# One PSUM tile for the 64-row jobs and another pairing of batches, in the last stage of an attention and spectral-mixing kernel

## The chip, the cores and the metric

The kernel runs on one core of one Trainium2 chip. The metric is the device time of one execution in microseconds (us); smaller is better. PE is the matmul engine, ACT and DVE are the two engines that read sums out of PSUM here, SyncE (SP) and GpSimd (POOL) issue the DMA transfers of this stage.

## The reference, cut to what matters

```python
# B = 8 batches, 8 heads x 64, S = 576 rows, D = 512
x   = attention_with_forget_decay(q, k, v, f)      # (B, S, D); cut
X   = np.fft.rfft(x, axis=1)[:, :64]               # 64 modes along the rows
Y   = X @ (w_r + 1j * w_i)                         # one D x D matrix per mode
u   = x + np.fft.irfft(Y, n=S, axis=1)
out = u + np.maximum(u @ w_ch, 0.0)                # float32, 9.44 MB
```

All weights have been read and all modes are done when the stage begins. What is left per row is `u = x + (inverse transform)` and `z = u @ w_ch`, which PE forms as sums in PSUM, the copy of u, `max(z, 0) + u`, and the store.

## The kernel before: the parts that the change and the argument touch

A batch has 576 rows: four blocks of 128 rows (`sb` 0 to 3) and a last one of 64 rows (`sb` 4). A *job* is one or two such blocks. I number the 20 jobs from 0.

```python
psPair = [{"u": psE, "z": psE}, {"u": psU}]     # "z" of the second pair: psX, added later

def start(n, tags="uz"):                        # PSUM tiles of job n, two banks each
    return [
        psPair[n % 2][tag].tile([128, 2, D], F32, tag=tag, name="p" + tag)
        for tag in tags
    ]

def wide(job):                                  # same block of two batches
    return len(job) == 2 and job[0][0] != job[1][0]

def emit_u(job, ps, u, split=False):            # ACT: u out of PSUM
    ...
        nc.scalar.copy(u[:, bs, :], ps[0][:, bs, :])

def emit_o(job, ps, u, o, pair, split=False):   # DVE, then SyncE's store
    for i in range(2 if split else 1):          # split: job 0 only, in two halves
        ...
        nc.vector.scalar_tensor_tensor(
            o[:, bs, :], ps[1][:, bs, :], 0.0, u[:, bs, :], ALU.max, ALU.add
        )
        b, sb = job[0]
        n_wide = 4 * (b // 2 - 1) + sb          # which wide job this is
        if sb == 4:
            ...                                 # single: two stores of 128 KB
        elif not wide(job):
            ...                                 # narrow pair: stored alone
        elif sb % 2 or n_wide < 2:              # wide: held for the next job,
            ...                                 #   but for the first two

jobs = []
for b in range(0, B, 2):
    if b == 0:
        jobs += [((c, sb), (c, sb + 1)) for c in (b, b + 1) for sb in (0, 2)]
    else:
        jobs += [((b, sb), (b + 1, sb)) for sb in range(4)]
    jobs.append(((b, 4),))

def late_rows(t, src):      # the last rows of Y, for u (t = 0) and for z (t = 1)
    keep(nc.vector.tensor_copy(yls[0][:, t, :], src))
    keep(nc.vector.tensor_copy(row_slot(0, t, H2, H4), yls[0][0:H4, t, :]))
    for b in (1, 2):        # 16 KB each, from one place in SBUF to another
        emit_moves(yls[0], H2, b, t, nc.sync)
    for b in (3, 4):
        emit_moves(yls[0], H2, b, t, nc.gpsimd)
... # batches 5 to 7: nc.gpsimd, afterwards

for n, job in enumerate(jobs):
    zs = terms(job, ps, 1, ...)                 # PE work of z of job n
    ...
        nxt = start(n + 1)
        us = terms(jobs[n + 1], nxt, 0, "xy")   # and of u of job n + 1
    ... # run zs and us, in an order that depends on the kind of job
        emit_u(jobs[n + 1], nxt, uo_n[0])
    emit_o(job, ps, *uo, n == 0)
```

The *small moves* in `late_rows` carry each batch's last rows of Y to the partitions where PE reads them. SyncE issues four of them, in the order: batch 1 for u, batch 2 for u, batch 1 for z, batch 2 for z.

The softmax here doesn't subtract the row's maximum and nothing guards it: scores larger than these inputs give would overflow.

## Time and profile before

| | before |
|---|---|
| time, median of 3 runs | 436.66 us (436.33 to 436.97) |
| the profiled run: time, span of its trace | 436.95 us, 435.2 us |
| last sum of the modes, where the stage starts (DVE writes YT) | 400.63 us |
| from there to the end of the span | 34.57 us |
| from there to the end of DVE's last step | 26.51 us |

Whole traces shift by a microsecond from one execution to the next ahead of the last stage (it starts between 400.11 and 401.81 in the traces of this study), so I count from the last write of YT wherever two traces are compared.

Of this stage the start, on DVE (columns: start, duration, engine, line, operation, output<-inputs, shape, count; in brackets the idle time before it and what ended it):

```profile
400.63 0.23 DVE L153 TENSOR_TENSOR YT<-A,Yacc 128x64 bf16<-128x64 f32 x1 [2.10 <-PE A L172]
...
403.99 2.52 DVE L1005 SCALAR_TENSOR_TENSOR uo<-pz,uo 128x512 f32<-128x512 f32 x3 [0.77 <-DMA yy<-yl]
406.71 1.23 DVE L1005 SCALAR_TENSOR_TENSOR uo<-pz,uo 128x1024 f32<-128x1024 f32 x1 [0.20 <-ACT uo L1000]
408.12 1.82 DVE L1005 SCALAR_TENSOR_TENSOR uo<-pz,uo 128x1024 f32<-128x1024 f32 x2 [0.19 <-PE pz L828]
410.48 4.67 DVE L1005 SCALAR_TENSOR_TENSOR os<-pz,us 128x1024 f32<-128x1024 f32 x4 [0.54 <-issue]
```

The first of the lower lines is jobs 0 and 1, the next two are jobs 2 and 3 (batch 1 alone) with the first single, the last is jobs 5 to 8. Job 2 waits only for ACT. The small moves do not appear as a wait after 403.99. In the DMA view of the stretch from 403.5 to 403.9, the third and the fourth small move of SyncE need 1.8 us from issue to landing (columns: tiles, queue, operation, count, size, median us to landing):

```profile
yy<-yl SPq DMA_DIRECT2D x2, 16.0 KB, 1.8
```

The same view from 402 to 407 has GpSimd's moves of the same size beside them:

```profile
yy<-yl POOLq DMA_DIRECT2D x10, 16.0 KB, 3.1
yy<-yl SPq DMA_DIRECT2D x4, 16.0 KB, 1.8
```

### The profile page before, as it was taken

Reading aid. Unit: us, or ns where it says so; the run is one execution under the profiler, and the core shown is the slowest. Engines: PE = TensorE matmul, PEld = TensorE weight load, DVE = VectorE, ACT = ScalarE, POOL = GpSimd, SP = SyncE. Lnnn points to the kernel's source line nnn. Section 1 sums busy time; section 2 is a strip of 40 time slices with the busy share of each in tenths; the row PEclk is TensorE's granted clock in tenths of the full one; section 3 lists DMA queues with packets and bytes.
Section 4 is the critical chain, followed back from the end, with each engine's and each line's share of the span. In section 5 each row is a group of like instructions: output and inputs, shape, how many; then the busy total and the mean of one; then the engine's idle time right before and its main releaser. Section 6 shows DMA issues by size and latency. Waiting matters only on the chain.

```text
span 435.2 us, 12314 instructions
## 1 busy us (share of the span) xinstructions
PE 368.1 (85%) x5313; PEld 249.7 (57%) x5313; DVE 263.7 (61%) x659; ACT 224.4 (52%) x339; POOL 126.8 (29%) x198
## 2 busy tenths in 40 slices
PE   3787799999987879778787788799999998899881
PEld 2454566776666666566565666656665555454540
DVE  5797888876555655555557568533332665553892
ACT  2887488774526454365462646134434443631781
POOL 8333332333233233232333222223223223200400
PEclk9996899996558665586565869589999999989997
DMA  8999999999999999999999999999999999995797
GB/s 184 234 235 241 234 236 238 235 212 236 234 215 236 225 224 237 210 238 233 214 237 211 212 211 212 211 211 211 211 211 211 212 210 211 211 211 100 253 367 274
DMA packets 50982, 97.38 MB, mean 224 GB/s; under 512 B 3792, under 2 KB 12976, under 8 KB 50928
## 3 DMA queue, kind: packets, MB, share of 16 engines
q0 software_dynamic: 46560, 86.09, 100.9%
q1 hardware_dynamic: 4368, 10.51, 6.7%
q8 instruction: 41, 0.67, 0.6%
q14 instruction: 13, 0.11, 0.1%
HBM read 163.73 MB, written 9.44 MB: 398 GB/s over the span
## 4 chain that ended last, share of the span: by engine, by line
PE 35%; DMA 26%; ACT 12%; DVE 10%; issue 4%; SPq 0%; DVEq 0%; POOL 0%; ACTq 0%
DMA wb<-in_moe_w_i_dram 25%; ACT E L576 8%; PE pav L614 7%; PE ps L569 7%; PE A L188 6%; PE tp L307 5%; PE px L657 2%; PE vp L541 2%; DVE QTs L322 2%; ACT KT L320 2%; ACT VT L326 2%; DVE XT L671 1%; DVE os L1005 1%; DVE E L591 1%; PE px L682 1%
## 5 line engine op out<-in xcount | busy, mean ns | idle before, releaser
L576 ACT ACTIVATE E<-ps 128x1024 bf16<-128x1024 f32 (+1 forms) x128 | 101.5, 851 | 26.1 <-PE ps L569 15.4
L93 POOL DMA_DIRECT2D wb<-in_moe_w_r_dram x64 | 42.5, 664 | 128.9 <-PE A L188 25.1
L188 PE MATMUL A<-XT,wb 128*128 128x16 bf16 x1984 | 69.9, 181 | 8.2 <-DMA wb<-in_moe_w_i_dram 3.8
L188 PEld LDWEIGHTS <-wb 128*128 128x128 bf16 x1984 | 63.5, 100 | 22.8 <-issue 11.9
L569 PE MATMUL ps<-QTs,KT 64*128 64x64 bf16 (+4 forms) x384 | 60.2, 334 | 16.6 <-ACT E L576 14.7
L93 POOL DMA_DIRECT2D wb<-in_moe_w_i_dram x64 | 42.3, 661 | 77.5 <-DMA wb<-in_moe_w_i_dram 32.5
L614 PE MATMUL pav<-va,E 128*128 128x65 bf16 (+1 forms) x1088 | 57.1, 214 | 3.2 <-DVE x_all L636 2.6
L614 PEld LDWEIGHTS <-E 128*128 128x128 bf16 (+1 forms) x1088 | 47.0, 118 | 16.9 <-issue 7.0
L591 DVE TENSOR_TENSOR E<-E,trimask 128x256 bf16<-128x256 bf16 (+2 forms) x128 | 36.9, 303 | 20.0 <-ACT E L576 19.8
L326 ACT COPY VT<-tp 128x640 bf16<-128x640 bf16 (+1 forms) x32 | 23.2, 761 | 33.4 <-PE tp L307 33.4
L867 ACT CAST XW<-pxw 128x512 bf16<-128x512 f32 x36 | 20.7, 586 | 35.9 <-PE pxw L860 28.3
L569 PEld LDWEIGHTS <-KT 64*128 64x128 bf16 x384 | 19.4, 100 | 33.6 <-issue 22.8
L860 PE MATMUL pxw<-wch,yy 128*128 128x512 bf16 x144 | 36.0, 388 | 0.0
L320 ACT COPY KT<-tp 128x640 bf16<-128x640 bf16 (+1 forms) x32 | 21.9, 749 | 26.0 <-PE tp L307 25.8
L910 ACT CAST XW<-pB 128x512 bf16<-128x512 f32 x36 | 21.0, 585 | 25.4 <-PE pB L828 25.3
L909 DVE CAST x_all<-pA 128x512 bf16<-128x512 f32 x36 | 24.9, 692 | 14.2 <-PE pA L828 12.5
L322 DVE COPY QTs<-tp 128x640 bf16<-128x640 bf16 (+1 forms) x32 | 23.4, 767 | 14.3 <-PE tp L307 14.0
L636 DVE TENSOR_TENSOR x_all<-pav,rcp 128x384 bf16<-128x384 f32 x64 | 29.1, 455 | 0.9
L625 DVE RECIPROCAL rcp<-pav 128x6 f32<-128x6 f32 x64 | 12.1, 189 | 25.1 <-PE pav L614 24.3
L828 PEld LDWEIGHTS <-ident_bf 64*64 64x64 bf16 (+1 forms) x348 | 15.7, 108 | 17.9 <-issue 9.3
L153 DVE TENSOR_TENSOR YTe<-A,Yacc 128x128 bf16<-128x128 f32 x16 | 5.9, 367 | 33.3 <-PE A L188 33.3
L541 PE MATMUL vp<-ident_bf,VT 128*128 128x128 bf16 x160 | 18.4, 261 | 4.6 <-DVE QTs L322 3.9
(142 smaller groups left out, 617.4 us busy)
## 6 DMA issues: line engine op xcount, KB each, us to landing
wb<-in_moe_w_r_dram POOLq DMA_DIRECT2D x62, 512.0 KB, 16.7
wb<-in_moe_w_i_dram POOLq DMA_DIRECT2D x62, 512.0 KB, 17.3
stv<-in_v_dram POOLq DMA_DIRECT2D x10, 576.0 KB, 15.2
out_dram<-os SPq DMA_DIRECT2D x10, 512.0 KB, 4.5
stk<-in_k_dram POOLq DMA_DIRECT2D x11, 288.0 KB, 15.3
stq<-in_q_dram POOLq DMA_DIRECT2D x11, 288.0 KB, 15.1
wx<-in_v_dram POOLq DMA_DIRECT2D x5, 576.0 KB, 15.4
out_dram<-uo SPq DMA_DIRECT2D x3, 512.0 KB, 3.6
```

Of the source, the lines that this page charges most:

```text
L93: keep(nc.gpsimd.dma_start(dst, src))
L188: ins = nc.tensor.matmul(A[:, eb, mi, :], lhsT=w_of(mi, eb * 128), rhs=x_of(m), start=(i == 0), stop=(i == len(terms) - 1),)
L320: nc.scalar.copy(rows(KTs[pr % 2][:, :, 0:S]), tv)
L322: ins = nc.vector.tensor_copy(rows(QT[pr][:, :, :]), tv)
L326: nc.scalar.copy(rows(VTs[pr % 2][:, :, 0:S]), tv)
L541: nc.tensor.transpose(vp[:, sc, :, :].rearrange("p b d -> p (b d)"), VTs[s // 2 % 2][:, h, sc * 128 : (sc + 1) * 128], ident_bf[:, :],)
L569: nc.tensor.matmul(ps[:, b, o : o + n], lhsT=KTs[pr % 2][bs, h, jb * 128 : (jb + 1) * 128], rhs=QT[pr][bs, h, jb * 128 + c0 : jb * 128 + c ...
L576: nc.scalar.activation(E[:, :, piece * 512 : piece * 512 + w], ps[:, :, 0:w], ACT.Exp, scale=scale,)
L591: nc.vector.tensor_tensor(dg, dg, tr, ALU.mult)
L614: nc.tensor.matmul(pav[64 * half : 64 * half + w, slot, :], lhsT=E[:, b, c : c + (w - 1) * st + 1 : st], rhs=va[:, jb, b, :], start=(n == ...
L636: nc.vector.tensor_tensor(xo, pi, ri, ALU.mult)
L860: nc.tensor.matmul(pxw[:, :], lhsT=xT[:, eb, i * 128 : (i + 1) * 128], rhs=wch[:, eb, :], start=(eb == 0), stop=(eb == NDC - 1),)
```

## The change

It has two intents. A single job needs 64 rows of two batches, that is, one bank for u and one for z: both fit in one two-bank tile, and the z tiles are left to the other jobs. And the pairing is shifted, so that the batches stored by themselves, in narrow pairs, are the first and the last (0 and 7) in place of the first two.

```diff
-        def start(n, tags="uz"):
-            return [
-                psPair[n % 2][tag].tile([128, 2, D], F32, tag=tag, name="p" + tag)
-                for tag in tags
-            ]
+        def bank(tag, n):
+            return psPair[n % 2][tag].tile([128, 2, D], F32, tag=tag, name="p" + tag)
+
+        def start(n):
+            u = bank("u", n)
+            if len(jobs[n]) == 1:
+                return [u[:, 0:1, :], u[:, 1:2, :]]
+            return [u, bank("z", sum(len(j) == 2 for j in jobs[:n]))]
...
-                n_wide = 4 * (b // 2 - 1) + sb
+                n_wide = 4 * ((b - 1) // 2) + sb
...
         for b in range(0, B, 2):
             if b == 0:
-                jobs += [((c, sb), (c, sb + 1)) for c in (b, b + 1) for sb in (0, 2)]
+                jobs += [((b, sb), (b, sb + 1)) for sb in (0, 2)]
+            if b < B - 2:
+                jobs += [((b + 1, sb), (b + 2, sb)) for sb in range(4)]
             else:
-                jobs += [((b, sb), (b + 1, sb)) for sb in range(4)]
+                jobs += [((b + 1, sb), (b + 1, sb + 1)) for sb in (0, 2)]
             jobs.append(((b, 4),))
```

So the order before is two jobs of batch 0, two of batch 1, single, then three times four wide jobs and a single. After, it is two jobs of batch 0, three times four wide jobs and a single, two jobs of batch 7, single. Job 2 is now the first wide job, of batches 1 and 2.

## The prediction

> **What bounds the kernel now.** I read the trace from its end. The change touches only the last stage, in which 20 *jobs* turn sums in PSUM into output rows. Job by job PE fills two PSUM tiles, u and z; ACT copies u to SBUF (L1000); DVE computes max(z,0)+u (L1005); SyncE's queue stores the result. A *wide* job takes a 128-row block of two batches and stores only at every second job (1 MB at once, but for the first two wide jobs, which store 512 KB each); a *narrow pair* takes two blocks of one batch (512 KB, stored alone); a *single* takes the last 64 rows of two batches (2 x 128 KB). The stage starts at 404 us of a 435.2 us span. An instruction-order comparison of the two programs shows that nothing before it moves.
>
> First view: engines and DMA in half-microsecond stretches (columns: PE, PEld, DVE, ACT, POOL busy, granted clock, DMA share, GB/s).
> ```profile
> 405.00:405.50 0.50, 0.50 (x10) 0.31 (x10) 0.49 (x2) 0.00 (x0) 0.50 (x2) 1.00 0.35 76
> 405.50:406.00 0.50, 0.50 (x14) 0.49 (x10) 0.50 (x1) 0.34 (x1) 0.50 (x2) 1.00 0.89 313
> ...
> 411.00:411.50 0.50, 0.32 (x8) 0.01 (x1) 0.50 (x1) 0.50 (x2) 0.00 (x0) 1.00 1.07 410
> ...
> 419.00:419.50 0.50, 0.50 (x14) 0.30 (x8) 0.50 (x1) 0.33 (x1) 0.00 (x0) 1.00 0.54 143
> ...
> 427.50:428.00 0.50, 0.00 (x0) 0.00 (x0) 0.00 (x0) 0.00 (x0) 0.00 (x0) 1.00 1.04 418
> ...
> 432.00:432.50 0.50, 0.00 (x0) 0.00 (x0) 0.00 (x0) 0.00 (x0) 0.00 (x0) 0.50 0.63 230
> 432.50:433.00 0.50, 0.00 (x0) 0.00 (x0) 0.00 (x0) 0.00 (x0) 0.00 (x0) 0.50 0.09 33
> ```
> DMA is full from 405.5 to about 432.5, and after 427.2 no engine computes: the last 5.3 us are stores draining. Second view, the store queue's own waits, says the same: the program's closing step waits for a store.
> ```profile
> SPq L1141 <- DMA out_dram<-uo: 2.6, 1, 2.6
> ```
> Third view: the groups of the stage, and DVE's timeline.
> ```profile
> L1005 DVE SCALAR_TENSOR_TENSOR os<-pz,us 128x1024 f32<-128x1024 f32 x12 | 14.1, 1220 | 1.3 <-issue 0.7 <-ACT us L1000 0.4
> L1000 ACT COPY us<-pu 128x1024 f32<-128x1024 f32 x12 | 11.9, 1015 | 3.4 <-PE pu L828 3.2
> L1005 DVE SCALAR_TENSOR_TENSOR uo<-pz,uo 128x512 f32<-128x512 f32 x6 | 4.0, 684 | 0.8 <-DMA yy<-yl 0.8
> ```
> ```profile
> 415.09 0.69 DVE L1005 SCALAR_TENSOR_TENSOR uo<-pz,uo 128x512 f32<-128x512 f32 x1
> 415.93 1.23 DVE L1005 SCALAR_TENSOR_TENSOR os<-pz,us 128x1024 f32<-128x1024 f32 x1
> 417.36 3.49 DVE L1005 SCALAR_TENSOR_TENSOR os<-pz,us 128x1024 f32<-128x1024 f32 x3 [0.20 <-ACT us L1000]
> 420.76 0.68 DVE L1005 SCALAR_TENSOR_TENSOR uo<-pz,uo 128x512 f32<-128x512 f32 x1
> ```
> DVE is nearly full too: four wide jobs and a single take 5.67 us (415.78 to 421.44) for 2.36 MB, that is 416 GB/s, the rate at which DMA drains. So two resources are balanced, and the stores, being last, set the end.
>
> **What the Trainium skill says.** "DMA: Bandwidth & Descriptors", section "Where 436 GB/s comes from", gives 435 GB/s as the ceiling of the ports between SBUF and DMA, and about 358 for HBM per core; the stores here run at 393 to 426, so the trace sides with the first and leaves no spare rate. The same page, "Latency and other measured facts", gives some 0.6 us to the first byte of such a store; here the first is issued at 404.71 and data flows in earnest from 405.5, and in an idle stretch the store issued at 418.76 reaches full rate at 420: I take 1.0 us. "PSUM — Partial Sum Buffer", section "Specifications (TRN2)": a bank holds 512 FP32 per partition. So a tile of this stage (1024 FP32) is two banks, and the pool is four such tiles, two u and two z. "Perfetto Trace Analysis", "Optimization Strategy", says that a bubble that repeats can mean too few PSUM buffers; the 0.2 us gaps after each single agree.
>
> **The change part by part.**
> (1) *A single in one tile.* Before, it took its u tile and its z tile of the rotation and used half of each. After, its u half and z half lie in the two banks of one u tile, and z tiles rotate over wide jobs and narrow pairs only. Removed: the wait of the next job's z matmuls for an old DVE step. Added, as the instruction order shows: the single's z matmuls wait for ACT's copy of its u half (the same tile), and the u matmuls of the job two later wait for DVE's step of the single, not for ACT's copy.
> Before, from the single's end at 415.78 to the start of the second job after it, 417.36, is 1.58 us. After: the DVE end, then PE's u matmuls 0.43 + 0.25 us until the last result is in (eight 64x64 matmuls start within 0.43 us in the timeline), ACT's copy 1.02 us and some 0.1 us of signalling: 1.8 us. The z half's own wait costs nothing: PE is over 0.5 us ahead of DVE there. So each single costs **+0.2 us**, three times with jobs behind it: DVE's end moves from 427.1 to about 427.7.
> (2) *Other pairing.* The job list keeps 20 entries, the same matmuls, the same two shapes of DVE step (15 of 1.22 us, 6 of 0.68) and the same store packets; the first single moves from fifth to seventh place, two narrow pairs from the third and fourth place to the two before the last single. Compute sums do not change. Avoided is the 0.54 us gap behind the first single (DVE idle 409.94 to 410.48): the first six big jobs and a single now end at about 412.4 and not 412.9.
> (3) *Release of bytes*, the part that reaches the path. Before, jobs 2 and 3 store 512 KB each at 408.0 and 409.4, the single follows at 410, jobs 5 and 6 store at 411.8 and 412.9: never dry. After, jobs 2 and 3 still store 512 KB each at about those times, but the fifth job only holds its rows; the next release is the sixth job's megabyte at about 411.75 (three DVE steps of 1.22 after 408.1, which waits for job 2). From the GB/s column, job 1 has drained by about 409.4; jobs 2 and 3 as two stores of 256 KB each at the 375 GB/s seen at 413 to 415 take 1.4 us each, to 412.2. The megabyte, issued at 411.9, flows from 412.9: **0.7 us of a dry queue.** Later on, release runs ahead of the drain in both; after's last jobs free 512 KB each, 512 KB earlier than before at the 18th job, but the queue has some 2.1 MB to go when DVE ends (5.3 us at 410), so an earlier release there only waits longer. Gained: the half-empty stretch at 418.7 to 419.7 (share 0.54 in one half microsecond), where before waits for the second job of a pair: about 0.3 us.
> Sum on the store path: +0.7 - 0.3 = +0.4 us; (1) is hidden, since +0.6 us of compute lies under a 5.3 us drain. I shade this to **+0.1 us**, since the dry stretch rests on a 0.7 us difference of estimates, and the edit may win a few tenths in places that I treat as equal. So 436.66 + 0.1, about 436.8.
>
> **The rivals.**
> *A: PSUM waits are what costs, and the tile saved shows at the end.* For it: PE and DVE show gaps at each single. Against it: the gaps sum to some 1 us, and stores still run 5.3 us after the last DVE step. It could give -0.5 to -1 us, and only if DVE's gain lets stores start sooner early in the stage: 435.7 to 436.2.
> *B: the smaller last stores help.* With 512 KB freed at the 18th job in place of 1 MB at the 19th, the queue could run empty less at the end. Against it: DMA is at 393 to 426 GB/s from 426.5 to 431. Worth 0 to -0.3 us.
> *C: batch 2's late rows come too late.* Job 2 now needs the rows of batches 1 and 2, moved by four small DMAs of which the last is issued at 403.6 and, at 1.8 us, lands at about 405.4 to 406.2. PE, in order, would stall before job 2's z. Before needs half of them there. If it lands at 406.2 it just fits (z of job 2 can start at 405.3, DVE takes it at 406.7); 0.5 us later, everything after moves: +0.5 us.
> *D: the new wait (1) is larger than I think and DVE falls behind DMA*: a stall of 1 us at each single would make the stage DVE-bound, +1 to +2 us. The order comparison shows the wait, so this has some weight.
>
> **Range and chances.** The stage touched is 31 us, and the stores' 9.44 MB at 410 GB/s alone take 23.0 us, against 27 used: the whole room for a gain is 4 us, part of it slow 64-row stores that stay. A 2% change is 8.7 us, out of reach of any rival. The three runs spread by 0.6 us. A and B at best give -1, D at worst +2; eight in ten: 435.8 to 437.7.
>
> **What would show it.** Right: the same time up to 404; DVE's last step at 427.3 to 428; four-job-and-single cycle 5.8 to 5.9 us; a stretch of low GB/s at 412 to 413; no low stretch at 419 except the slow 64-row store; last data within 0.5 us of 432.5; PE or ACT, not DVE, waiting at the job two after each single. Wrong: stores draining less than 3 us behind the last DVE step (D), PE waiting for the small moves at 406 (C), or the last data before 431.7 (A, B).

## The result, and the profile after

| | before | after |
|---|---|---|
| time, median of 6 runs | 436.82 us (436.33 to 437.03) | 438.79 us (437.47 to 439.56) |
| ratio after / before | | 1.0046, 95% interval 1.0029 to 1.0064 |
| the profiled run: time, span | 436.95, 435.2 us | 439.56, 437.8 us |
| last YT to the end of the span | 34.57 us | 36.90 us |
| last YT to the end of DVE's last step | 26.51 us | 30.62 us |

Ratios here and below are the mean time of one kernel's fast runs over that of the other's fast runs of the same rounds, so they are not quite the ratio of the medians beside them. The changed kernel is slower by about 2.0 us (0.46% of 436.8). That is within 2%, as predicted, but beyond the range of 435.8 to 437.7.

First view: the groups of the last stage, with the idle time ahead of them (for before see the prediction).

```profile
L1008 DVE SCALAR_TENSOR_TENSOR os<-pz,us 128x1024 f32<-128x1024 f32 x12 | 14.3, 1219 | 3.8 <-ACT us L1003 2.2 <-PE pz L828 1.7
L1003 ACT COPY us<-pu 128x1024 f32<-128x1024 f32 x12 | 11.8, 1017 | 6.2 <-PE pu L828 5.7 <-PE pz L828 0.5
```

The steps cost what they did (1219 against 1220 ns), but DVE idles 3.8 us ahead of them where it idled 1.3, and ACT 6.2 where it idled 3.4. The extra time is waiting, and it points at PE. Second view, DVE's timeline:

```profile
400.90 0.23 DVE L153 TENSOR_TENSOR YT<-A,Yacc 128x64 bf16<-128x64 f32 x1 [2.42 <-PE A L172]
...
404.26 2.42 DVE L1008 SCALAR_TENSOR_TENSOR uo<-pz,uo 128x512 f32<-128x512 f32 x3 [0.77 <-DMA yy<-yl]
408.35 1.22 DVE L1008 SCALAR_TENSOR_TENSOR os<-pz,us 128x1024 f32<-128x1024 f32 x1 [1.67 <-PE pz L828]
409.79 1.23 DVE L1008 SCALAR_TENSOR_TENSOR os<-pz,us 128x1024 f32<-128x1024 f32 x1 [0.21 <-ACT us L1003]
411.20 1.23 DVE L1008 SCALAR_TENSOR_TENSOR os<-pz,us 128x1024 f32<-128x1024 f32 x1 [0.19 <-ACT us L1003]
412.91 1.22 DVE L1008 SCALAR_TENSOR_TENSOR os<-pz,us 128x1024 f32<-128x1024 f32 x1 [0.48 <-ACT us L1003]
414.35 0.69 DVE L1008 SCALAR_TENSOR_TENSOR uo<-pu,uo 128x512 f32<-128x512 f32 x1 [0.22 <-PE pz L828]
414.96 1.21 DVE L1008 SCALAR_TENSOR_TENSOR os<-pz,us 128x1024 f32<-128x1024 f32 x1
416.82 3.48 DVE L1008 SCALAR_TENSOR_TENSOR os<-pz,us 128x1024 f32<-128x1024 f32 x3 [0.64 <-ACT us L1003]
420.55 0.69 DVE L1008 SCALAR_TENSOR_TENSOR uo<-pu,uo 128x512 f32<-128x512 f32 x1 [0.25 <-PE pz L828]
```

The first wide job (408.35) waits 1.67 us for PE's z. The next three come 1.4 to 1.7 us apart instead of back to back. Later the steady cycle is there, single to single 414.35 to 420.55, with its two small gaps. Third view, the chain of waits of this stretch (start, duration, what):

```profile
403.21 0.30 DVE yy L1075
403.51 0.34 SPq L823
403.85 0.04 issue
403.89 3.92 DMA yy<-yl
407.81 0.04 issue
407.86 0.40 PE pz L828 x2
```

Read it from the bottom: PE's two last matmuls of z of job 2 began when SyncE's fourth small move landed. It was issued at 403.89 and took 3.92 us, not 1.8. PE's own timeline names the same wait:

```profile
405.85 0.38 PE L828 MATMUL pz<-yy,BIl 64*64 64x512 bf16 x2
407.86 0.40 PE L828 MATMUL pz<-yy,BIl 64*64 64x512 bf16 x2 [1.63 <-DMA yy<-yl]
```

Fourth view, stretches around the wait (columns as in the prediction; the third column from the end is the granted clock of PE):

```profile
404.00:406.30 2.30, 2.09 (x24) 0.78 (x21) 2.04 (x3) 1.84 (x3) 2.30 (x6) 1.00 0.44 120
406.30:407.85 1.55, 0.00 (x0) 0.00 (x0) 0.39 (x1) 0.23 (x1) 1.25 (x3) 1.00 0.43 121
407.85:408.90 1.05, 1.04 (x20) 0.75 (x23) 0.55 (x1) 0.15 (x1) 0.00 (x0) 0.98 0.89 324
408.90:412.30 3.40, 3.40 (x38) 2.65 (x30) 3.00 (x3) 2.30 (x3) 0.00 (x0) 0.50 0.87 331
```

PE stands still from 406.30 to 407.85, and from 408.9 to 412.3 it is busy all the time (3.40 of 3.40 us) at half clock. The three jobs after the wait come late too. For the first of them, job 3, the clock is not the reason: ACT's copy for it starts before the clock falls, as soon as PE has formed its u:

```profile
408.75 1.01 ACT L1003 COPY us<-pu 128x1024 f32<-128x1024 f32 x1 [2.21 <-PE pu L828]
```

Fifth view, what it does to the stores:

```profile
413.50:414.00 0.50, 0.42 (x12) 0.29 (x9) 0.50 (x1) 0.49 (x2) 0.00 (x0) 1.00 0.05 16
414.00:414.50 0.50, 0.50 (x12) 0.24 (x3) 0.28 (x2) 0.50 (x1) 0.00 (x0) 1.00 0.00 0
414.50:415.00 0.50, 0.19 (x2) 0.00 (x0) 0.50 (x2) 0.12 (x1) 0.00 (x0) 1.00 0.06 25
...
434.50:435.00 0.50, 0.00 (x0) 0.00 (x0) 0.00 (x0) 0.00 (x0) 0.00 (x0) 0.50 0.89 238
435.00:435.50 0.50, 0.00 (x0) 0.00 (x0) 0.00 (x0) 0.00 (x0) 0.00 (x0) 0.50 0.47 148
```

The store queue runs dry for 1.5 us, and the last data come at about 435.4, 34.5 us after YT; before it was 432.6, 32.0 us after. The store still closes the program (the queue's last wait is now 2.1 us, against 2.6). So the theory is: **the pairing makes an early job need the small move that is issued last, and this move can land 2 us late.**

### The profile page after: what moved, and what is told of

Read it like the earlier page. It is cut to its first block, busy times and chain, and to the rows that moved or that the text cites. A ratio compares the mean times of both kernels' runs of the same rounds, so it can differ in the third digit from the quotient of the medians.

```text
span 437.8 us, 12312 instructions
## 1 busy us (share of the span) xinstructions
PE 357.6 (82%) x5313; PEld 244.7 (56%) x5313; DVE 263.7 (60%) x659; ACT 224.0 (51%) x339; POOL 126.8 (29%) x198
## 4 chain that ended last, share of the span: by engine, by line
DMA 40%; PE 28%; ACT 10%; DVE 6%; issue 4%; ACTq 0%; POOL 0%; SPq 0%; DVEq 0%
DMA wb<-in_moe_w_i_dram 39%; ACT E L576 7%; PE pav L614 6%; PE ps L569 5%; PE A L188 5%; PE tp L307 4%; PE pu L828 2%; DVE QTs L322 2%; ACT KT L320 2%; PE px L657 2%; PE vp L541 1%; PE px L682 1%; DVE E L591 1%; ACT VT L326 1%; PE pz L828 1%
## 5 line engine op out<-in xcount | busy, mean ns | idle before, releaser
L188 PE MATMUL A<-XT,wb 128*128 128x16 bf16 x1984 | 70.9, 182 | 15.2 <-DMA wb<-in_moe_w_i_dram 10.4
L569 PE MATMUL ps<-QTs,KT 64*128 64x64 bf16 (+4 forms) x384 | 56.2, 311 | 20.5 <-ACT E L576 18.6
L614 PE MATMUL pav<-va,E 128*128 128x65 bf16 (+1 forms) x1088 | 53.6, 206 | 3.1 <-DVE x_all L636 2.6
L614 PEld LDWEIGHTS <-E 128*128 128x128 bf16 (+1 forms) x1088 | 43.9, 112 | 18.8 <-issue 9.5
L828 PEld LDWEIGHTS <-ident_bf 64*64 64x64 bf16 (+1 forms) x348 | 16.6, 109 | 18.4 <-issue 9.3
L153 DVE TENSOR_TENSOR YT<-A,Yacc 128x128 bf16<-128x128 f32 (+1 forms) x17 | 6.0, 352 | 25.0 <-PE A L188 20.8
```

The costliest lines, as they stand in the source:

```text
L188: ins = nc.tensor.matmul(A[:, eb, mi, :], lhsT=w_of(mi, eb * 128), rhs=x_of(m), start=(i == 0), stop=(i == len(terms) - 1),)
L569: nc.tensor.matmul(ps[:, b, o : o + n], lhsT=KTs[pr % 2][bs, h, jb * 128 : (jb + 1) * 128], rhs=QT[pr][bs, h, jb * 128 + c0 : jb * 128 + c ...
L614: nc.tensor.matmul(pav[64 * half : 64 * half + w, slot, :], lhsT=E[:, b, c : c + (w - 1) * st + 1 : st], rhs=va[:, jb, b, :], start=(n == ...
L828: return nc.tensor.matmul(p, lhsT=lhsT, rhs=rhs, start=first, stop=not first, skip_group_check=True)
```

## The experiments

The main theory, called M, is the late move. Its rivals: the waits that the single's one tile brings; the bytes that the fifth job holds back, which starve the stores; and the shape of the last stores. I made 15 runs in four calls, each call on another chip (e1 to e4; e0, e5, e6, e8; e9, e10, e11, e13; e14 to e16); each call shares its own runs of the kernel before, whose medians were 436.49, 436.44, 436.20 and 437.17 us. The last call's runs of before are spread most, 436.00 to 438.00.

| run | median us (range) | ratio to before, 95% | PE waited for a move in its trace |
|---|---|---|---|
| e0: after, again | 438.06 (436.32 to 438.74) | 1.0029, 1.0012 to 1.0047 | no |
| e1: one tile only | 436.93 (436.32 to 437.33) | 1.0006, 0.9992 to 1.0020 | no |
| e2: pairing only | 437.54 (435.81 to 438.79) | 1.0017, 0.9994 to 1.0039 | no |
| e3: after, moves dealt anew | 436.76 (436.11 to 437.44) | 1.0000, 0.9984 to 1.0016 | no |
| e8: after, the move put later | 440.32 (439.13 to 441.86) | 1.0086, 1.0067 to 1.0106 | 2.15 us |
| e10: before, narrow pairs last | 436.65 (436.31 to 436.99) | 1.0007, 0.9995 to 1.0020 | no |
| e11: before, four wide jobs not held | 436.37 (435.15 to 436.73) | 0.9995, 0.9981 to 1.0009 | no |
| e4: e3, four wide jobs not held | 436.07 (435.57 to 436.61) | 0.9987, 0.9972 to 1.0001 | no |
| e5: e2, moves dealt anew | 436.61 (435.01 to 437.58) | 1.0000, 0.9984 to 1.0016 | no |
| e6: e5, four wide jobs not held | 435.85 (435.18 to 436.91) | 0.9987, 0.9974 to 1.0000 | no |
| e13: e5, no wide job held | 436.52 (435.49 to 437.95) | 1.0001, 0.9986 to 1.0016 | no |
| e9: after, first store whole | 435.72 (435.42 to 436.41) | 0.9989, 0.9976 to 1.0002 | no |
| e14: before, first store whole | 436.50 (434.80 to 437.37) | 0.9986, 0.9964 to 1.0009 | no |
| e15: after, first store later | 437.45 (436.32 to 438.77) | 1.0019, 0.9995 to 1.0042 | no |
| e16: e6, first store whole | 435.80 (435.02 to 436.56) | 0.9976, 0.9957 to 0.9995 | no |

**e1 and e2: one part at a time.** e1 is the kernel before with the new `bank` and `start` of the diff alone; e2 is the changed kernel with the old `start`.

> The pairing of before, the single's two halves in one u tile as after. Theory M (batch 2's late rows arrive too late for the third job) and theory H (the fifth job only holds its rows, so the store queue runs dry): this run has neither, so 436.6 to 437.2, the drain hiding a DVE that ends 0.5 to 1.5 us later. Theory P (the single's new waits are what costs): 438 to 439, nearly the whole loss. In all theories the cycle of four wide jobs and a single grows from 5.67 to about 6.2 us.

> The pairing of after, two tiles for the single as before. M: 438.2 to 438.8, with PE waiting 1 us or more for a late move before the third job's z. H: 437.5 to 438, with a low-GB/s stretch around 413. P: 436.8, no loss.

e1 is as fast as before (1.0006), so the tile is not the loss. Yet its DVE is slower; these are two singles and the jobs between them in its timeline:

```profile
415.62 0.69 DVE L1008 SCALAR_TENSOR_TENSOR uo<-pu,uo 128x512 f32<-128x512 f32 x1 [0.24 <-issue]
416.23 1.21 DVE L1008 SCALAR_TENSOR_TENSOR os<-pz,us 128x1024 f32<-128x1024 f32 x1
418.08 3.49 DVE L1008 SCALAR_TENSOR_TENSOR os<-pz,us 128x1024 f32<-128x1024 f32 x3 [0.64 <-ACT us L1003]
421.81 0.69 DVE L1008 SCALAR_TENSOR_TENSOR uo<-pu,uo 128x512 f32<-128x512 f32 x1 [0.24 <-issue]
```

The cycle is 6.19 us (421.81 minus 415.62), against 5.67 before, and DVE ends 27.87 us after YT, against 26.51. These 1.36 us vanish under the drain of the stores. With the pairing alone (e2), the six times were 435.81, 436.25, 437.46, 437.62, 438.35 and 438.79: two below the median of before (436.49), the slowest like the changed kernel. The median lies below M's forecast of 438.2 to 438.8, and the profile happened to fall on the fastest run, which shows no wait. The interval of e2 (0.9994 to 1.0039) reaches below 1, so e2 alone does not prove a loss; with e1 free of it, this points to the pairing, and to a loss that does not strike in each execution.

**e3: the late move made early.** Batch 2's moves become SyncE's first and third, and batch 1's go to GpSimd; as many moves on each queue as before, and no job is changed.

```diff
-            for b in (1, 2):
+            for b in (2, 3):
                 emit_moves(yls[0], H2, b, t, nc.sync)
-            for b in (3, 4):
+            for b in (1, 4):
                 emit_moves(yls[0], H2, b, t, nc.gpsimd)
```

> The changed kernel with the small moves dealt out anew: batches 2 and 3 on SyncE's queue and 1 and 4 on GpSimd's, so that the second half of batch 2 is issued 0.6 us earlier, ahead of the first store. M: the PE wait of 1.6 us goes, 437.0 to 437.5. H: still dry at 413 after the fifth job, 438. P: no change, 438.8.

The loss is gone: 1.0000, no run above 437.44. Jobs 2 to 5 run back to back on DVE:

```profile
404.60 2.42 DVE L1008 SCALAR_TENSOR_TENSOR uo<-pz,uo 128x512 f32<-128x512 f32 x3 [0.77 <-DMA yy<-yl]
406.93 4.66 DVE L1008 SCALAR_TENSOR_TENSOR os<-pz,us 128x1024 f32<-128x1024 f32 x4
```

The tile, the held bytes and the last stores are all still in this kernel; only the moves differ.

**e0 and e8: the same kernel again, and the move made later on purpose.** In e8 the fourth move goes into SyncE's queue behind job 0's two stores.

```diff
             for b in (1, 2):
-                emit_moves(yls[0], H2, b, t, nc.sync)
+                if (b, t) != (2, 1):
+                    emit_moves(yls[0], H2, b, t, nc.sync)
...
             emit_o(job, ps, *uo, n == 0)
+            if n == 0:
+                emit_moves(yls[0], H2, 2, 1, nc.sync)
```

> The changed kernel unaltered, on the chip of the runs beside it, for comparison and for a second trace. M: 438 to 439; the trace shows either a PE wait of 1 us or more for a late move, or, if the lateness is a matter of chance, none and a time near 436.8. A constant loss with no such wait would speak against M.

> The changed kernel with one move, that of batch 2's second half, put behind the first job's two stores on SyncE's queue: issued about 1.8 us later. M: PE waits for it in every run, job 3's DVE step begins at 409 to 410, and the time is 439.5 to 441 with little spread. P and H: no change from the changed kernel, 438.8.

e8 loses more, 1.0086, as the late move has it. Its PE line, and the stretches around it:

```profile
409.30 0.64 PE L828 MATMUL pz<-yy,BIl 64*64 64x512 bf16 x2 [2.15 <-DMA yy<-yl]
```
```profile
406.80:409.30 2.50, 0.35 (x7) 0.00 (x1) 0.00 (x0) 0.52 (x1) 0.35 (x1) 0.93 0.83 299
409.30:412.00 2.70, 2.70 (x22) 1.31 (x24) 1.98 (x2) 1.01 (x1) 0.00 (x0) 0.50 0.11 43
```

Here the clock falls to half near the end of the wait, at about 409.0, and the stores dry up (43 GB/s). e0: the six times of the unaltered changed kernel run from 436.32 to 438.74, and the profile fell on 436.32. So there are traces of one program with the move late (the one above) and with the move on time (this one):

```profile
400.13 0.22 DVE L153 TENSOR_TENSOR YT<-A,Yacc 128x64 bf16<-128x64 f32 x1 [2.43 <-PE A L172]
...
403.49 2.42 DVE L1008 SCALAR_TENSOR_TENSOR uo<-pz,uo 128x512 f32<-128x512 f32 x3 [0.77 <-DMA yy<-yl]
405.82 4.66 DVE L1008 SCALAR_TENSOR_TENSOR os<-pz,us 128x1024 f32<-128x1024 f32 x4
410.71 0.69 DVE L1008 SCALAR_TENSOR_TENSOR uo<-pu,uo 128x512 f32<-128x512 f32 x1 [0.24 <-PE pz L828]
...
427.19 0.69 DVE L1008 SCALAR_TENSOR_TENSOR uo<-pu,uo 128x512 f32<-128x512 f32 x1
```
```profile
408.90:412.30 3.40, 2.89 (x40) 1.34 (x39) 3.16 (x4) 2.08 (x4) 0.00 (x0) 1.00 1.01 385
```

| us after the last YT | after, move late | after, move on time (e0) | difference |
|---|---|---|---|
| DVE starts job 2 | 7.45 | 5.69 | 1.76 |
| jobs 2 to 5 on DVE, start to end | 5.78 | 4.66 | 1.12 |
| DVE's last step ends | 30.62 | 27.75 | 2.87 |
| span ends | 36.90 | 34.47 | 2.43 |

The two terms add up to 2.88 us, which is what DVE ends later; 0.4 us of it disappear in the drain. Of the 1.12 us, 0.27 come before job 3 (1.44 us from the start of job 2 to that of job 3, against 1.17 in e0), which ACT's copy above shows not to be the clock's; the other 0.85 fall in the stretch at half clock. The fourth move was issued at 403.12 in e0 and landed 1.8 us later. The stretch from 408.9 to 412.3 runs at full clock here, and in each of the 13 other experiments' traces that show no wait the mean clock from 403 to 426 is 1.00. Half clock in this stretch goes with the wait, in both traces that have one.

**e10 and e11: the rivals on the kernel before.** e10 deals the last two batches as narrow pairs, so that stores get smaller at the end; e11 stores the first four wide jobs at once, as e4 and e6 do for the other job list.

```diff
# e10
-            else:
+            elif b < B - 2:
                 jobs += [((b, sb), (b + 1, sb)) for sb in range(4)]
+            else:
+                jobs += [((c, sb), (c, sb + 1)) for c in (b, b + 1) for sb in (0, 2)]
# e11, and e4 and e6 on top of e3 and e5
-                elif sb % 2 or n_wide < 2:
-                    rs = slice(sb % 2 if n_wide < 2 else 0, sb % 2 + 1)
+                elif sb % 2 or n_wide < 4:
+                    rs = slice(sb % 2 if n_wide < 4 else 0, sb % 2 + 1)
```

> The kernel before with the last pair of batches stored alone, by halves (the intent of the pairing, without its early use of batch 2). Rival B (smaller last stores help): 0.3 us or more under before. Drain theory (two megabytes are queued when DVE ends, so nothing changes): within 0.2 us of before.

> The kernel before with the first four wide jobs stored at once, not two. The same edit gained 0.6 us on each of two kernels with the new pairing. If holding rows costs wherever the queue is short, 436.0 here too; if it matters only where the wide jobs come first, no change, 436.5.

> As the run with the moves dealt anew, and the first four wide jobs (not two) store 512 KB each at once. M: little more than that run, within 0.3 us of it. H: the dry stretch goes too, 0.7 to 1 us less than that run, 436.5 or below. P: 438.8.

Smaller last stores are worth nothing (e10, 1.0007). Holding fewer bytes is worth nothing in the kernel before (e11), where narrow pairs fill that time, and at most about 0.6 us in the new order: e4 against e3 is 0.9987 against 1.0000, and 0.0013 times 436.5 is 0.57 us, with intervals that overlap.

**e5, e6 and e13: the new pairing with the old tiles.**

> The pairing of after, two tiles for the single, and the moves dealt anew. M: the 1 us by which the pairing alone was slower than before goes, and the spread of its times (435.8 to 438.8) shrinks to 1 us: 435.8 to 436.5, as fast as before or faster. If the pairing has another cost (H), 437 or above.

> As the run with the pairing, two tiles and the moves dealt anew, and four wide jobs stored at once. H: 0.5 us less than that run, about 435.5. If the dry stretch is worth nothing with two tiles, the same.

> The new pairing, two tiles for the single, moves dealt anew, and all twelve wide jobs stored at once in 2 KB pieces. If the gain of storing early is all at the start, as fast as with four (0.13% under before). If 2 KB pieces drain slower (375 against 410 GB/s as estimated in the prediction), 1 us slower than that; if holding costs everywhere, faster still.

e5 equals e3 and e6 equals e4 to the fourth digit, though two tiles for a single let DVE end sooner: in e5 its last steps are these, and end at 426.15, against 428.99 in e3 (whose stage starts later by 1.1 us or so).

```profile
421.95 0.69 DVE L1005 SCALAR_TENSOR_TENSOR uo<-pz,uo 128x512 f32<-128x512 f32 x1
423.06 3.09 DVE L1005 SCALAR_TENSOR_TENSOR uo<-pz,uo 128x1024 f32<-128x1024 f32 x3 [0.41 <-PE pu L828]
```

DVE's end does not matter while the stores drain behind it. With no wide job held (e13), all wide stores are cut into rows of 2 KB pieces; it comes out at 1.0001, where four jobs gave 0.9987. The two are from different calls, so this is a hint only that small pieces for all the stores cost more than the holding saves.

**e9, e14 and e15: the first store.** Why is the move late? My first idea was the first store, which is issued about a microsecond behind it. e9 stores job 0 whole: one store with 4 KB pieces, issued some 0.5 us later (1.6 us after the fourth move in e9, 1.1 in the late trace). e14 is the same on the kernel before. e15 keeps 2 KB pieces and two stores, but issues them in the other order, so that the first goes out later.

```diff
# e9 and e14
-            emit_o(job, ps, *uo, n == 0)
+            emit_o(job, ps, *uo)
# e15: both DVE halves of job 0 first, then the stores
+                for i in (1, 0):
+                    keep(nc.sync.dma_start(... [:, i : i + 1, :], o[:, i : i + 1, :]))
```

> The changed kernel with the first job's store left whole: issued 0.6 us later, in 4 KB pieces, so that no store data moves before about 406. If the late move of batch 2 is caught behind the first store's data (race theory), it now always lands in some 1.8 us, no PE wait, and the time is 436.5 to 437.3 with a spread of 1 us. If the move is slow for another reason, PE still waits in some runs and the median stays at 438 or above.

> Control: the kernel before with the first job's store left whole, as in the run that was the fastest so far. Before never needs batch 2's late rows early. If that edit only removed the race, no change here, 436.4. If whole 4 KB pieces drain faster by themselves, 0.3 to 0.5 us less, and that share is not the race's.

> The changed kernel with the first job's two half stores in the other order: the same pieces of 2 KB, but the first of them can only go after both DVE steps, 0.6 us later. Race theory: no PE wait, small spread, 435.7 to 436.7. If it was the size of the pieces that helped when the store was left whole: 438, with the wait still there in some runs.

e9 takes the loss away without touching the moves: five runs, none above 436.41. But e15, which also lets the first store go later, still had two runs of six at 438.74 and 438.77, like the slow runs of the changed kernel (a run of before took 438.00, though); its profiled run (437.47) shows no wait. So a later first store alone is not shown to be the cure. e14 is not clearly different from before. This group was inconclusive on the mechanism.

**What the traces show of the late move.** The kept traces say more than this group. The fourth move was late in three of them, and two of these have the early jobs of the old pairing: e10 (3.50 us) and e11 (3.32). There no early job needs it, PE did not wait, the clock stayed at 1.00 from 403 to 426, and nothing was lost. So the change did not make the move late; it made the late move count. Nor does the issue of the first store decide it: that follows the move's by 1.09 or 1.10 us in the three late traces, and by 1.09 in before, e0, e1 and e2, where the move took 1.8 us. The store's data start at 405.84 in the late trace, when 15 of the move's 16 packets (1 KB each) have run, by 405.39. The sixteenth packet had to wait, and beside it ran one packet of 16 KB, which the DMA view lists by the kind `instruction`, and which is none of the program's own transfers (here from 405.24 to 405.30 and from 406.72 to 406.80; columns: queue, kind, packets, MB, share of 16 engines):

```profile
q8 instruction: 1, 0.02, 159.3%
q1 hardware_dynamic: 1, 0.00, 9.7%
```

159.3% of 16 engines for 0.06 us is 1.53 us of one engine: the packet lasts from 405.25 to 406.78. The second line is the move's sixteenth packet, which starts at 406.77. The packet records of the traces give this for all:

| trace | move issued | `instruction` packet starts, after that | it ends | move's last packet starts | issue to landing |
|---|---|---|---|---|---|
| after (late) | 403.89 | 1.36 us | 406.78 | 406.77 | 3.92 us |
| e10 (late) | 403.27 | 1.28 us | 405.73 | 405.72 | 3.50 us |
| e11 (late) | 403.80 | 1.29 us | 406.02 | 406.01 | 3.32 us |
| e0 | 403.12 | 1.59 us | 406.15 | 404.56 | 1.84 us |
| before | 403.62 | 1.59 us | 406.48 | 405.06 | 1.82 us |

In the 11 other traces (all but e8, which issues this move elsewhere) the `instruction` packet starts 1.57 to 2.40 us after the issue of SyncE's fourth move, and the move takes 1.79 to 1.88 us. In all 16 traces the move's packets start 1.24 to 1.25 us after its issue, and where nothing holds one back the last starts at 1.45 at most. So the move was late in each trace where the `instruction` packet started among the move's packets, and in no other; one packet of the move then started only at its end. This is read from the traces; no run moved the `instruction` packet.

**e16: all together.** The new pairing, two tiles for a single, the moves of e3, four wide jobs not held, the first store whole.

> The new pairing, two tiles for the single, the moves dealt anew, four wide jobs stored at once, and the first store whole. If the gains add: 435.3 to 435.7, below the run without the last edit (0.13% under before). If moves and first store cure the same race: 435.8.

It is the one kernel whose interval lies below 1: 0.9976 (0.9957 to 0.9995), about 1 us faster than before. One interval of 15 may miss by chance, and e16 shares its call with the most spread runs of before, so this is a hint. By the ratios to before, which come from other calls, it also lies below the changed kernel (1.0046 and 1.0029). It is still within 2% of both.

## Why the prediction was wrong, point by point

**The end of the stage, right.** The stores closed the program in both kernels, and DVE's later end did not count as long as it was small: e1 shows 1.36 us of it for a ratio of 1.0006, and e3 and e5 show the same from the other side. With the move late, DVE ends 4.1 us later than before and the span 2.3, so the drain hides only part of that.

**Step (1), the tile: right that it is hidden, a size off.** From a single's end to the start of the second job after it the changed kernel takes 1.78 us (415.04 to 416.82); predicted were 1.8, before 1.58. But "The z half's own wait costs nothing" is wrong: there are 0.22 to 0.25 us of idle ahead of each single that follows wide jobs. The cycle is 6.2 us, not 5.8 to 5.9: a single costs 0.5 us of DVE's time, not 0.2.

**Step (2), the pairing: right in its sum, wrong in what it overlooked.** The matmuls and DVE steps are the same; the loss is in what job 2 waits for, which stood under rival C.

**Step (3), the release of bytes: wrong.** With the move on time there is no stretch of 0.7 us without stores. The working had job 2 end at 408.1 and the next three follow 1.22 us apart, to 411.75. In e0 jobs 2 to 5 start at 405.82 and end at 410.48, back to back, 1.17 us each (4.66 / 4). That is 1.27 us sooner; 0.5 us of it is the earlier start of this trace's stage (400.13 against 400.63), the other 0.8 us more than fill the 0.7 us that were to be dry. The lowest half microsecond between 410 and 413.5 in e0 is

```profile
411.00:411.50 0.50, 0.09 (x6) 0.04 (x7) 0.50 (x2) 0.00 (x0) 0.00 (x0) 1.00 0.88 324
```

The dry stretch at 413.5 to 415 in the late trace looks like this step come true, but it is a consequence of the wait: it is absent from the same program when the move is on time. The half-empty stretch at 419 is gone, as foreseen: e0 moves 401 to 426 GB/s from 418 to 419.5.

**Rival C, the step that failed.** The sum and the range left this wait out, and it is the loss. The prediction named the cause, the wait and the place: "PE waiting for the small moves at 406". It sized it by "If it lands at 406.2 it just fits" and "0.5 us later, everything after moves: +0.5 us". Two terms were too small. The landing was taken from the median of SyncE's moves, 1.8 us, and was 3.92 us, with one packet behind the `instruction` packet. At 1.8 us it would have come at 405.69, and PE was ready for it at 406.23 (407.86 less the wait of 1.63): 0.54 us to spare, as the prediction had it, but the move was 2.1 us late. And the cost of a wait was taken to be its length; but jobs 2 to 5 took 1.12 us longer, most of it (0.85) at half clock, from 408.9 to 412.3. Together DVE ran 2.87 us late and the span 2.43 us. Not every execution is hit: e0's and e2's fastest runs show no wait and no loss. With the move on time the change costs about nothing, as e3 measures (436.76 us, 1.0000). That the predicted 436.8 is so near to e3 is luck in part, since the dry stretch of 0.7 us in its sum is not there.

**Rivals A, B and D fell.** A and B gave no gain (e1, e10); D's stall is 0.5 us for each single (the cycle grows from 5.67 to 6.2 us), hidden.

**What stays open.** Why the `instruction` packet comes 1.36 us after the move's issue in one execution and 1.59 in another of the same program is not shown, nor on which DMA engine a packet runs: the traces do not name it. From the move's last packet to its landing it takes 0.9 to 1.0 us in the three late traces and 0.3 in e0; I do not know why. GpSimd's moves behind the fourth are slow as well (3.2 us for one issued at 404.41 in the trace of before), and I did not sort out which of them stood behind the `instruction` packet and which behind stores. It is also not shown that the slow runs without a trace are those in which the move was late, nor why e9 had no slow run. And SyncE's second store takes 0.9 to 2.0 us to issue in some traces, 0.3 in others, with and without the late move; I did not find out why.

## What to carry to other kernels

When a job list is reordered, write down for each early job every input it needs and when the last of them arrives, the small transfers too. Give a transfer that was never waited for the worst landing of its size in the trace, not the median of its queue: before's own trace had moves of 16 KB at 1.8 us on one queue and a median of 3.1 on the other, so a move with half a microsecond of slack had none. Look in the DMA view for packets that are not yours. Look at the spread of the runs before believing one profile (one program gave 436.3 and 439.6 us here), and count a PE wait in a dense stretch at more than its length: here 1.76 us of delay became 2.87.

## What the Trainium skill lacked or had wrong

- "TensorE: Matmul & The Clock Gate", section "Part 1: The HAM clock gate", under "What's actually happening", lets the clock fall to half after at least one idle window of about 3.4 us and puts that window at 3413 ns. Here PE was idle for 1.6 us only (2.15 in e8). In the first of these traces the clock fell 1 us after PE had resumed, while it was busy; in e8 it fell 0.3 us before the wait ended. The length agrees: half clock lasted 3.4 us in both (408.9 to 412.3 in the first). So an idle time of about half a window (1.6 of 3.4 us) was followed by half clock in one trace, and one of 0.6 window in the other.
- "DMA: Bandwidth & Descriptors", section "Latency and other measured facts", gives about 2 us as the fixed cost of a DMA. Moves of 16 KB inside SBUF took 1.6 to 2.0 us here when nothing stood in their way, but 3.3 to 3.9 us when one of their packets stood behind an `instruction` packet. The section has no figure for a small transfer beside other traffic.
- The same page, section "Where 436 GB/s comes from", has transfers between SBUF and HBM bound by 358 GB/s on the HBM side, and names no condition for it. The stores of this kernel, which has one core at work, run above that for microseconds at a time, 418 GB/s in the prediction's lines of before. Other pages of the skill allow a core that streams alone more, so it is this passage that wants the condition.
